# Three fp32 loads in one queue, w_in's first quarter in two loads, and q turned at other places in a decayed-attention and MLP kernel

## The chip, the cores and the metric

The kernel runs on one core of a Trainium2 chip. The time is the device time of one execution in microseconds, given as the median of several runs. TensorE is called PE here, VectorE DVE, ScalarE ACT, GpSimd POOL and SyncE SP, as in the profile.

## The reference

Attention with a decay per head and no softmax, then a two-layer MLP with the snake activation. B, H, S, D = 4, 8, 768, 64; the MLP is 512 to 2048 to 512.

```python
for b in range(nb):                                   # blocks of 64 positions
    intra = einsum('bhic,bhjc->bhij', qb, kb) * Dmask # lam^(i-j) for i >= j
    intra = einsum('bhij,bhjd->bhid', intra, vb)
    inter = einsum('bhid,bhde->bhie', qb * lam_pow, kv_state)
    out[:, :, sl] = intra + inter
    kv_state = lam_block * kv_state + einsum('bhsd,bhse->bhde', kb * rev_pow, vb)
x = out.transpose(0, 2, 1, 3).reshape(B * S, H * D)
h = x @ w_in
g = h + sin(alpha * h)**2 / (alpha + 1e-09)
return g @ w_out
```

## The kernel before

The 768 positions are cut into six chunks of 128 positions (t = 0 to 5). A chunk holds 4 batches × 128 positions = 512 rows. For each chunk the kernel does the attention, which ends in `xt[t]` (the rows' 512 features, turned, in bf16), and then the MLP, group g = t: 16 hidden blocks of 128 features (`hidden(g, f)`, f = 0 to 15, four matmuls each into one PSUM bank `hps`), the activation, and the projection to the output (`project(g, m, part)`: batch m, a quarter of the 16 blocks; `queue_units` puts the projections in a list, and `run(n)` issues the next n of them). There is no scheduler: every engine's order is the order in which the program issues. PE's work of three stages is interleaved by hand: while group g's hidden blocks run, the attention of chunk g + 1 and the projections of earlier groups are put between them.

In `hidden`, ACT makes the sine of a block (L465) and then mostly its square (L470). `squarer(g, f)` says who squares: in group 0 DVE does so for some f, in `finish` (L478). `finish` also makes `gall` from the square and the bank (L479, DVE), and with that the bank is free for a later block. In group 1 the blocks 4 to 14 go round three banks, so that block 12 takes the bank that block 9 had.

Chunk 0 is done with one block of 128 positions, without a state (`scores1`, L307; `outs`, L318). The later chunks have two blocks of 64 and a state: `states` (L378), `update`, `scores` (L398), `masks` (DVE, L405), `outputs_first` (L412), `outputs` (L437), `leave` (L444). q and k have to be turned first: on PE with an eviction by ACT or DVE (`turn`, L282 to L286, one batch; `turns_pair`, L296 to L301, two), or from chunk 2 on mostly by a transposing DMA in SP's queue (`turn_by_dma`).

Loads: nearly everything comes through POOL's software queue, cast from fp32 to bf16 on the way (`load`, `load_w_in`, `load_w_out`). Each such load takes over the landing semaphore of the one eight places ahead in POOL's order, and POOL waits for that one's landing before it issues. Only three pieces for the start come in fp32 through hardware queues: k of batch 0 (`raw["k0"]`), q of batch 0 (`q0`) and k of batch 1 (`k1`) of chunk 0. DVE casts the two k (L525, L533) and multiplies q by the powers `Rq` (L526). `mask_128` makes the table `C0` of the decay, one half per call (L529). Between the steps PE runs fillers (`spin`, L131).

For groups 1 and on, `feed(g)` and `slots(g)` give what is put at each hidden block: feed's steps come ahead of `hidden(g, i)`, slots' steps behind it, and then come the projections and `finish`.

Of the kernel before, what the change touches and what calls it, by code (L numbers as in the profile page):

```python
# [15 lines left out]
def kernel(  # L16
# [11 lines left out]
    nc = tc.nc  # L28
    P = nc.NUM_PARTITIONS
# [28 lines left out]
    def bank(nm, n, dtype=FP32):  # L58
        return psum.tile([P, 512 if dtype is FP32 else 1024], dtype, name=nm, tag=f"b{n}")
# [3 lines left out]
    AB = (4, 5, 6, 7)  # L63
# [7 lines left out]
    qn, kn, vn = {}, {}, {}  # L71
# [4 lines left out]
            d[t] = p.tile([P, B, H, D], BF16, name=nm)  # L76

    raw = {}
    for nm, eng in (("k0", nc.sync), ("q0", nc.scalar), ("k1", nc.sync)):
        raw[nm] = rawp.tile([P, H, D], FP32, name=f"raw_{nm}")  # L80
        eng.dma_start(out=raw[nm][:], in_=NAT[nm[0]][1][int(nm[1]), :, 0:T, :].rearrange("h p e -> p h e"))
    alpha_fp = consts.tile([NFC, P], FP32, name="alpha_fp")
# [4 lines left out]
    def load_w_in(i, w0=0, w1=512):  # L87
        w = slice(512 * i + w0, 512 * i + w1)
        nc.gpsimd.dma_start(out=w_in_sb[i][:, :, w0:w1], in_=moe_w_in[:, w].rearrange("(c p) g -> p c g", p=P))
# [25 lines left out]
    for hs in (slice(0, HP), slice(HP, H)):  # L115
        nc.gpsimd.dma_start(out=vn[0][:, 3, hs, :], in_=v[3, hs, 0:T, :].rearrange("h p e -> p h e"))
    load_w_in(0, 0, P)
    load_w_in(0, P, 2 * P)
    load_w_in(0, 2 * P, 512)
    for i in range(1, 4):  # L120
        load_w_in(i)

# [5 lines left out]
    def spin(n, bk, cols=256):  # L128
        ps = bank("hps", bk)
        for _ in range(n):  # L130
            nc.tensor.matmul(out=ps[:, 0:cols], lhsT=fill[:, 0:P], rhs=fill[:, 0:cols], start=True, stop=True)  # L131
# [79 lines left out]
    V, G, A = nc.vector, nc.gpsimd, nc.scalar  # L211
# [17 lines left out]
    def home(t, blk):  # L229
        return SB[2 if blk else t % 2]  # L230
# [7 lines left out]
    def decay_k(t, b0, b1):  # L238
        if t not in kdec:
            kdec[t] = kdp.tile([P, B, H, D], BF16, name="kdec")  # L240
        R = later["R64" if t else "R128"]
        o = int(turned_by_one(t, b0 // 2))
        nc.gpsimd.tensor_tensor(out=kdec[t][:, b0:b1, :, :], in0=kn[t][:, b0:b1, :, :],  # L243
                                in1=R[:, o:o + H].unsqueeze(1).unsqueeze(3).broadcast_to([P, b1 - b0, H, D]),
                                op=ALU.mult)
# [32 lines left out]
    def turn(t, nm, b, n, eng):  # L278
        src, u = (kn, 0) if nm == "k" else (qn, 1)
        ps = bank("T_ps", n, BF16)[:].rearrange("p (n c i) -> p n c i", n=2, c=HP)[:, u]  # L280
        for hp in range(HP):
            nc.tensor.transpose(out=ps[:, hp, :], in_=src[t][:, b, 2 * hp:2 * hp + 2, :], identity=iden[:])  # L282
        if eng is nc.scalar:
            eng.copy(out=both[t][:, u, b, :, :], in_=ps)  # L284
        else:
            eng.tensor_copy(out=both[t][:, u, b, :, :], in_=ps)  # L286
# [44 lines left out]
    def states1(t, pr, n):  # L331
        ps = bank("KV0_ps", n)[:].rearrange("p (u c d) -> p u c d", u=2, c=HP)
        for h in range(2 * H):
            half, m = where(1, pr, h)
            nc.tensor.matmul(out=ps[halves(half), m // HP, m % HP, :], lhsT=head(kdec, t, pr, h),
                             rhs=vn[t][:, 2 * pr + h // H, h % H, :], start=True, stop=True)
        new_state(1, pr, ps, "first")
# [4 lines left out]
    def decay_state(n, pr):  # L342
        nc.gpsimd.tensor_tensor(out=pair(SD, pr), in0=pair(S_of[n], pr), op=ALU.mult,  # L343
                                in1=L64[:, pr].unsqueeze(1).unsqueeze(3).broadcast_to([P, 2, HP, D]))

    def cast_state(n, pr, dst):
        nc.gpsimd.tensor_copy(out=pair(dst, pr), in_=pair(S_of[n], pr))  # L347
# [102 lines left out]

    def squarer(g, f):
        if g == 0:
            return V if f in (1, 3, 5, 7, 9, 13) else A
        return A

    H0 = (0, 1, 2, 3, 5, 6, 7, 4, 0, 1, 3, 5, 0, 1, 5, 0)
# [1 line left out]
    def hidden(g, f, between=None):  # L458
        hps = bank("hps", H0[f] if g == 0 else (0, 5, 4, 2)[f] if g == 1 and f < 4 else AB[0] if g == 1 and f == 15 else AB[f + 1] if g == 2 and f < 2 else HB[(f + 2) % 3] if g == 1 else HB[(16 * g + f + 1) % 3])
        w = w_in_sb[f // 4]  # L460
        for c in range(NDC):
            nc.tensor.matmul(out=hps[:], lhsT=w[:, c, (f % 4) * P:(f % 4 + 1) * P],  # L462
                             rhs=xt[g][:, c, :], start=(c == 0), stop=(c == NDC - 1))
        s_sb = mlps.tile([P, GRP], BF16, name="s_sb")
        nc.scalar.activation(out=s_sb[:], in_=hps[:], func=ACTF.Sin, scale=alpha_sb[:, f:f + 1])  # L465
        if between:
            between()
        s2 = mlps.tile([P, GRP], BF16, name="s2")
        if squarer(g, f) is A:
            nc.scalar.activation(out=s2[:], in_=s_sb[:], func=ACTF.Square)  # L470
        elif squarer(g, f) is G:
            nc.gpsimd.tensor_tensor(out=s2[:], in0=s_sb[:], in1=s_sb[:], op=ALU.mult)
        hps_of[g, f] = (hps, s_sb, s2)
# [48 lines left out]
    new_xt(0)  # L522
    new_turned(0)
    spin(4, 0, 512)
    nc.vector.tensor_copy(out=kn[0][:, 0, :, :], in_=raw["k0"][:])  # L525
    nc.vector.tensor_tensor(out=qn[0][:, 0, :, :], in0=raw["q0"][:], op=ALU.mult,  # L526
                            in1=Rq[:].unsqueeze(2).broadcast_to([P, H, D]))
    def mask_128(hd):
        nc.vector.tensor_tensor(out=C0[:, hd], in0=tri[:].unsqueeze(1).broadcast_to([P, HP, T]),  # L529
                                in1=NE[:, hd].unsqueeze(2).broadcast_to([P, HP, T]), op=ALU.mult)  # L530

    mask_128(0)
    nc.vector.tensor_copy(out=kn[0][:, 1, :, :], in_=raw["k1"][:])  # L533
    mask_128(1)
    turn(0, "k", 0, 4, A)
    spin(2, 3)
# [68 lines left out]
    def run(n):  # L605
        for _ in range(min(n, len(behind))):
            behind.pop(0)()
# [3 lines left out]
    for f in range(NFC):  # L611
        hidden(0, f)
        if f in (1, 10):
            states1(0, f // 10, 2 if f == 10 else 4)
        if f == 10:
            decay_k(1, 0, 2)
            decay_state(1, 0)
            cast_state(1, 0, home(1, 0))
            load(1, "q", 2, 4)
            load_w_out(2)  # L620
            load_w_out(3)
            load(2, "v", 0, 2)
        if f in (11, 12):
            run(1)
        if f == 12:
            turns_pair(1, "k", 0, 4, (A, A))
            turn(1, "q", 0, 2, A)
            turn(1, "q", 1, 3, V)
        if f == 14:
            scores(1, (0,), (4, 2))  # L630
            masks(1, 0)
        if f == 15:
            run(1)
            states(1, (0,), (3, 4))
            finish(0, 14)
            update(1, 0, 0)
        if f != 14:
            finish(0, f)
# [33 lines left out]
    def slots(g):  # L672
        t = g + 1
        d = {i: [] for i in range(NFC)}
        if g == 1:
            at = dict(KV=5, F=9, O=12)
        else:
            at = dict(KV=4, F=8, O=12)
        d[at["KV"]] += [(states, t)]
        for n in range(4):  # L680
            d[at["KV"] + ((0, 0, 1, 2)[n] if g == 1 else n)] += [(update, t, n // 2, n % 2)]
        if g == 1:
            d[7] += [(turns_pair, 2, "q", 2, AB[0], (A, A))]
        else:
            d[at["F"]] += [(scores, t), (masks, t, 0)]
        d[at["F"] + (g > 1)] += [(masks, t, 1)]
        d[at["O"]] += [(outputs, t), (leave, t, 0)]
        d[at["O"] + (g > 1)] += [(leave, t, 1)]
        return d

    def feed(g):
        t = g + 1
        d = {i: [] for i in range(NFC)}
        if g == 1:
            d[2] += [(turn_by_dma, 2, 0, "k"), (pair_ready, 2, 1), (decay_state, 1, 0), (decay_state, 1, 1), (turn_by_dma, 2, 1, "k"), (turn_by_dma, 2, 0, "q")]
            d[7] += [(put_held,)]
            d[9] += [(scores, 2), (masks, 2, 0)]
        if t + 1 < NT:
            if g == 1:
                d[6] += [(new_chunk, 3)] + [(load, 3, nm, b, b + 2) for nm, b in (("v", 0), ("k", 0), ("v", 2))]  # L700
                d[7] += [(load, 3, nm, b, b + 2) for nm, b in (("k", 2), ("q", 0), ("q", 2))]
            else:
                a = 6 if g == 2 else 2
                d[a] += [(new_chunk, t + 1)] + [(load, t + 1, nm, b, b + 2) for nm, b in (("v", 0), ("k", 0), ("v", 2))]
                d[a + 2] += [(load, t + 1, nm, b, b + 2) for nm, b in (("k", 2), ("q", 0), ("q", 2))]
            d[12] += [(turn_by_dma, t + 1, 0, "k"), (turn_by_dma, t + 1, 1, "k")]
            d[13] += [(pair_ready, t + 1, 0)]
            d[14] += [(turn_by_dma, t + 1, 0, "q"), (turn_by_dma, t + 1, 1, "q")]
            d[15] += [(pair_ready, t + 1, 1)]
        return d  # L710
# [59 lines left out]
```

## Time and profile before

| | |
|---|---|
| median of 3 runs | 209.48 us (209.28 to 209.59) |
| the profiled execution | 209.52 us, of which the span is 207.7 us |
| granted PE clock | 1.0 |
| PE, DVE, ACT, POOL busy | 198.1, 132.5, 143.1, 108.0 us |
| chain that ended last | PE 75%, DMA 12%, POOL 8%, issue 2%, ACT 2% |
| POOL's software queue | 76,720 packets, 13.24 MB |

The profile is of one execution. Busy time is that of instructions on an engine; the share of the chain is what one sees when one follows the last instruction back, step by step, to what released it. In the rows of a timeline stand the start and the length in microseconds, engine, line, operation and tiles, and in brackets how long the engine stood idle ahead of it and for whom.

### The profile page before, as it was taken

Reading aid. Unit: us, or ns where it says so; the run is one execution under the profiler, and the core shown is the slowest. Engines: PE = TensorE matmul, PEld = TensorE weight load, DVE = VectorE, ACT = ScalarE, POOL = GpSimd, SP = SyncE. Lnnn points to the kernel's source line nnn. Section 1 sums busy time; section 2 is a strip of 40 time slices with the busy share of each in tenths; the row PEclk is TensorE's granted clock in tenths of the full one; section 3 lists DMA queues with packets and bytes.
Section 4 is the critical chain, followed back from the end, with each engine's and each line's share of the span. In section 5 each row is a group of like instructions: output and inputs, shape, how many; then the busy total and the mean of one; then the engine's idle time right before and its main releaser. Section 6 shows DMA issues by size and latency. Waiting matters only on the chain.

```text
span 207.7 us, 5323 instructions
## 1 busy us (share of the span) xinstructions
PE 198.1 (95%) x2203; PEld 97.9 (47%) x2233; DVE 132.5 (64%) x219; ACT 143.1 (69%) x240; POOL 108.0 (52%) x113
## 2 busy tenths in 40 slices
PE   7898998999998999999999999999999999999993
PEld 2563444554454544445445444444445444444462
DVE  6895996582897969968557968555867544444000
ACT  4897988323988799675776675776676787887121
POOL 8979959997989983999976940002000000000000
PEclk9999999999999999999999999999999999999999
DMA  7999999999999999599999929601101101110212
GB/s 144 157 159 207 206 160 181 179 183 156 155 264 111 146 151 176 37 170 158 137 149 194 171 60 157 150 0 54 50 3 54 50 0 50 52 54 0 101 60 94
DMA packets 99338, 24.60 MB, mean 118 GB/s; under 512 B 92002, under 2 KB 96370, under 8 KB 99314
## 3 DMA queue, kind: packets, MB, share of 16 engines
q0 software_dynamic: 76720, 13.24, 85.9%
q1 hardware_dynamic: 21552, 10.76, 25.2%
q10 hardware_dynamic: 1042, 0.26, 0.6%
q8 instruction: 17, 0.28, 0.5%
q14 instruction: 7, 0.06, 0.1%
HBM read 27.27 MB, written 6.29 MB: 162 GB/s over the span
## 4 chain that ended last, share of the span: by engine, by line
PE 75%; DMA 12%; POOL 8%; issue 2%; ACT 2%; POOLq 0%; ACTq 0%
PE ops L490 35%; PE hps L462 33%; DMA kn<-in_k_dram 4%; DMA w_out<-in_moe_w_out_dram 4%; DMA vn<-in_v_dram 3%; POOL kdec L243 3%; PE O_ps L412 2%; PE hps L514 2%; PE F_ps L398 1%; POOL qn L104 1%; PE KV_ps L378 1%; PE O_ps L437 1%; POOL kn L104 1%; ACT s_sb L465 1%; POOL qn L101 1%
## 5 line engine op out<-in xcount | busy, mean ns | idle before, releaser
L479 DVE SCALAR_TENSOR_TENSOR gall<-s,r_sb,hps 128x512 bf16<-128x512 bf16 x96 | 70.9, 744 | 43.7 <-ACT s L470 43.4
L462 PE MATMUL hps<-xt,w_in 128*128 128x512 bf16 x370 | 94.3, 379 | 1.5 <-DMA w_in<-in_moe_w_in_dram 0.4
L490 PE MATMUL ops<-w_out,gall 128*128 128x512 bf16 x352 | 90.5, 379 | 1.2 <-issue 0.3
L465 ACT ACTIVATE s_sb<-hps,alpha_sb 128x512 bf16<-128x512 f32 x96 | 65.3, 684 | 33.5 <-PE hps L462 33.1
L470 ACT ACTIVATE s<-s_sb 128x512 bf16<-128x512 bf16 x90 | 56.7, 630 | 2.8
L462 PEld LDWEIGHTS <-w_in 128*128 128x128 bf16 x384 | 36.5, 98 | 43.7 <-DMA w_in<-in_moe_w_in_dram 0.9
L490 PEld LDWEIGHTS <-gall 128*128 128x128 bf16 x368 | 34.7, 98 | 41.2 <-issue 0.9
L243 POOL TENSOR_TENSOR kdec<-kn,R 128x1024 bf16<-128x1024 bf16 x12 | 22.8, 1919 | 3.7 <-DMA kn<-in_k_dram 3.3
L347 POOL CAST sb<-S 128x512 bf16<-128x512 f32 x20 | 12.3, 621 | 20.8 <-DVE S L354 20.8
L343 POOL TENSOR_TENSOR SD<-S,L 128x512 f32<-128x512 f32 x16 | 16.8, 1050 | 8.9 <-DVE S L354 8.7
L444 DVE TENSOR_TENSOR xt<-O_ps,Etab 128x512 bf16<-128x512 f32 x20 | 12.8, 684 | 6.0 <-PE O_ps L437 6.0
L104 POOL DMA_DIRECT2D vn<-in_v_dram x12 | 14.0, 1173 | 0.0
L497 DVE COPY o_sb<-ops 128x512 f32<-128x512 f32 x15 | 10.3, 689 | 4.2 <-PE ops L490 4.1
L499 ACT COPY o_sb<-ops 128x512 f32<-128x512 f32 x8 | 4.6, 576 | 12.0 <-PE ops L490 12.0
L405 DVE TENSOR_TENSOR STm<-F_ps,C 128x512 bf16<-128x512 f32 x20 | 12.7, 683 | 0.2 <-PE F_ps L398 0.2
L354 DVE TENSOR_TENSOR S<-SD,KV_ps 128x512 f32<-128x512 f32 x16 | 10.8, 682 | 0.1
L131 PE MATMUL hps<-fill 128*128 128x256 bf16 (+1 forms) x30 | 8.1, 379 | 1.5 <-DVE fill L124 1.5
L104 POOL DMA_DIRECT2D qn<-in_q_dram x8 | 8.8, 1097 | 0.3 <-issue 0.3
L284 ACT COPY QKT<-T_ps 128x512 bf16<-128x512 bf16 x11 | 6.3, 587 | 3.5 <-PE T_ps L282 3.4
L104 POOL DMA_DIRECT2D kn<-in_k_dram x7 | 7.6, 1092 | 0.0
L412 PEld LDWEIGHTS <-sb 64*64 64x64 bf16 x320 | 4.3, 108 | 4.7 <-issue 4.7
L101 POOL DMA_DIRECT2D kn<-in_k_dram x5 | 6.2, 1234 | 0.0
(76 smaller groups left out, 114.3 us busy)
## 6 DMA issues: line engine op xcount, KB each, us to landing
out_dram<-o_sb SPq DMA_DIRECT2D x23, 256.0 KB, 2.1
vn<-in_v_dram POOLq DMA_DIRECT2D x11, 256.0 KB, 7.7
w_out<-in_moe_w_out_dram POOLq DMA_DIRECT2D x4, 512.0 KB, 11.1
w_in<-in_moe_w_in_dram POOLq DMA_DIRECT2D x3, 512.0 KB, 9.6
kn<-in_k_dram POOLq DMA_DIRECT2D x5, 256.0 KB, 7.6
qn<-in_q_dram POOLq DMA_DIRECT2D x5, 256.0 KB, 8.4
kn<-in_k_dram POOLq DMA_DIRECT2D x5, 240.0 KB, 7.3
qn<-in_q_dram POOLq DMA_DIRECT2D x5, 240.0 KB, 8.0
```

Of the source, the lines that this page charges most:

```text
L104: nc.gpsimd.dma_start(out=to, in_=by_head)
L243: nc.gpsimd.tensor_tensor(out=kdec[t][:, b0:b1, :, :], in0=kn[t][:, b0:b1, :, :], in1=R[:, o:o + H].unsqueeze(1).unsqueeze(3).broadcast_to ...
L343: nc.gpsimd.tensor_tensor(out=pair(SD, pr), in0=pair(S_of[n], pr), op=ALU.mult, in1=L64[:, pr].unsqueeze(1).unsqueeze(3).broadcast_to([P, ...
L347: nc.gpsimd.tensor_copy(out=pair(dst, pr), in_=pair(S_of[n], pr))
L354: nc.vector.tensor_tensor(out=S, in0=pair(SD, pr), in1=ps, op=ALU.add)
L405: nc.vector.tensor_tensor(out=st[:, hd], in0=att["F", t, pr, hd], op=ALU.mult, in1=of_mask(C64, t, pr, hd).unsqueeze(1).broadcast_to([P, 2 ...
L444: nc.vector.tensor_tensor(out=xview(t)[:, 2 * pr:2 * pr + 2, blk, :, :], in0=att["O", t, pr, blk], in1=Eb, op=ALU.mult)
L462: nc.tensor.matmul(out=hps[:], lhsT=w[:, c, (f % 4) * P:(f % 4 + 1) * P], rhs=xt[g][:, c, :], start=(c == 0), stop=(c == NDC - 1))
L465: nc.scalar.activation(out=s_sb[:], in_=hps[:], func=ACTF.Sin, scale=alpha_sb[:, f:f + 1])
L470: nc.scalar.activation(out=s2[:], in_=s_sb[:], func=ACTF.Square)
L479: nc.vector.scalar_tensor_tensor(out=gall[g][:, f, :], in0=s2[:], scalar=r_sb[:, f:f + 1], in1=hps[:], op0=ALU.mult, op1=ALU.add)
L490: nc.tensor.matmul(out=ops[:], lhsT=gall[g][:, f, m * P:(m + 1) * P], rhs=w_out_sb[part][:, f % 4, :], start=(f == 0), stop=(f == NFC - 1))
```

## The change

- The loads of k0, q0 and k1 are all issued on SP, in this order; q0 was issued on ACT.
- w_in's first quarter (512 columns) is loaded as 128 and 384 columns; it was 128, 128 and 256. POOL has one load less to issue, and each later one takes over the semaphore of another load than before.
- DVE casts k0 and k1 one right behind the other, ahead of the multiplication of q0; k1's cast stood between the two halves of the mask table.
- In group 0, block 1 is squared by ACT instead of DVE.
- q of chunk 1, batches 0 and 1, is turned behind hidden block 13 of group 0 instead of block 12, and both evictions are on DVE; the first was on ACT.
- q of chunk 2, batches 2 and 3, is turned by PE ahead of hidden block 7 of group 1 instead of behind it.

```diff
-    for nm, eng in (("k0", nc.sync), ("q0", nc.scalar), ("k1", nc.sync)):
+    for nm, eng in (("k0", nc.sync), ("q0", nc.sync), ("k1", nc.sync)):
...
     load_w_in(0, 0, P)
-    load_w_in(0, P, 2 * P)
-    load_w_in(0, 2 * P, 512)
+    load_w_in(0, P, 512)
...
         if g == 0:
-            return V if f in (1, 3, 5, 7, 9, 13) else A
+            return V if f in (3, 5, 7, 9, 13) else A
...
-    nc.vector.tensor_copy(out=kn[0][:, 0, :, :], in_=raw["k0"][:])
+    for b in range(2):
+        nc.vector.tensor_copy(out=kn[0][:, b, :, :], in_=raw[f"k{b}"][:])
     nc.vector.tensor_tensor(out=qn[0][:, 0, :, :], in0=raw["q0"][:], op=ALU.mult,
...
     mask_128(0)
-    nc.vector.tensor_copy(out=kn[0][:, 1, :, :], in_=raw["k1"][:])
     mask_128(1)
...
         if f == 12:
             turns_pair(1, "k", 0, 4, (A, A))
-            turn(1, "q", 0, 2, A)
+        if f == 13:
+            turn(1, "q", 0, 2, V)
             turn(1, "q", 1, 3, V)
...
-        if g == 1:
-            d[7] += [(turns_pair, 2, "q", 2, AB[0], (A, A))]
-        else:
+        if g > 1:
             d[at["F"]] += [(scores, t), (masks, t, 0)]
...
-            d[7] += [(put_held,)]
+            d[7] += [(put_held,), (turns_pair, 2, "q", 2, AB[0], (A, A))]
```

## The prediction

> **What bounds the kernel now.** I read the page first, then the chain of waits in order of time, then the timeline of the stretches where the chain is not TensorE.
>
> ```profile
> PE 198.1 (95%) x2203; PEld 97.9 (47%) x2233; DVE 132.5 (64%) x219; ACT 143.1 (69%) x240; POOL 108.0 (52%) x113
> ```
>
> TensorE (PE) is busy for 95% of the span, so what can be won is its idle time, and of that only what ends up on the chain. The chain view (start, length, what) runs through loads up to 43.77 and almost only through PE from there on:
>
> ```profile
> 35.22 8.51 DMA w_out<-in_moe_w_out_dram
> 43.77 1.02 PE ops L490 x4
> ```
>
> The third quarter of w_out is issued at 35.22 and lands at 35.22 + 8.51 = 43.73; PE starts on it at 43.77. The timeline shows PE's stops (in brackets the idle time before a row and what ended it):
>
> ```profile
> 20.34 6.22 PE L462 MATMUL hps<-xt,w_in 128*128 128x512 bf16 x27 [0.41 <-DMA w_in<-in_moe_w_in_dram]
> ...
> 31.74 0.62 PE L282 MATMUL T_ps<-iden,qn 128*128 128x128 bf16 x8 [0.57 <-DMA qn<-in_q_dram]
> ...
> 43.77 1.02 PE L490 MATMUL ops<-w_out,gall 128*128 128x512 bf16 x4 [0.18 <-DMA w_out<-in_moe_w_out_dram]
> ...
> 62.81 0.73 PE L398 MATMUL F_ps<-QKT 64*64 64x64 bf16 x64 [0.60 <-ACT QKT L299]
> ```
>
> Up to 43.77 PE waits three times, each time for a load of POOL's software queue: 0.41 + 0.57 + 0.18 = 1.16 us. What loses less than that before 43.77 is swallowed there, and what wins time there is lost again, as long as the third quarter of w_out lands when it does. So I asked the DMA view whether that landing can move, for 5.1 to 43.7 us, and for one microsecond with large and one with small packets:
>
> ```profile
> DMA  9999999999999999999999999999999999999999
> ...
> q0 software_dynamic: 26912, 6.82, 193.1%
> ```
> ```profile
> DMA packets 207, 0.21 MB, mean 209 GB/s; under 512 B 3, under 2 KB 207, under 8 KB 207
> ```
> ```profile
> DMA packets 1234, 0.16 MB, mean 157 GB/s; under 512 B 1234, under 2 KB 1234, under 8 KB 1234
> ```
>
> The 16 DMA engines are busy in every slice (all nines) and the software queue (q0) moves 6.82 MB in that time. It runs full, so a load lands when what is ahead of it has passed, not sooner for being issued sooner. **My reading: up to 43.77 the kernel is paced by the software queue, behind it by PE.**
>
> **The change part by part.**
>
> *One software load less.* The first quarter of w_in comes as 128 + 384 columns instead of 128 + 128 + 256. Bytes are the same; packets go from 512 + 512 to 512. From the two rows above, a packet costs the queue 1 us / 1234 = 0.81 ns at 130 bytes (0.16 MB / 1234) and 1 us / 207 = 4.83 ns at 1,014 bytes (0.21 MB / 207). A line through both rises 4.02 ns over 884 bytes and has a fixed part of 0.22 ns, so 512 fewer packets take 512 × 0.22 = 0.11 us off everything behind them. Bounds: -0.1 (nothing saved, and the larger block in the way of what is behind it) to 0.41 us (512 packets at the full price of a small one). I take 0.11 because both rows are of this queue running full; the landing at 43.73 then comes at 43.62.
>
> On POOL itself one issue goes:
>
> ```profile
> 9.35 3.04 POOL L89 DMA_DIRECT2D w_in<-in_moe_w_in_dram x4
> ...
> 13.28 0.74 POOL L89 DMA_DIRECT2D w_in<-in_moe_w_in_dram x1 [0.88 <-DMA vn<-in_v_dram]
> ...
> 15.68 3.77 POOL L243 TENSOR_TENSOR kdec<-kn,R 128x1024 bf16<-128x1024 bf16 x2
> ```
>
> In the program a software load waits for the landing of the one eight places ahead (it takes over its semaphore). The wait of 0.88 us for v stays, now ahead of the last quarter of w_in instead of the third, so POOL passes 13.28 as before with one issue less to do: kdec starts 0.74 us earlier, at 14.94, and the loads behind it are issued 0.74 us earlier. By the full queue that moves no landing. Price of the merge: the second block of 128 columns must wait for all 384.
>
> ```profile
> L89 POOL DMA_DIRECT2D w_in<-in_moe_w_in_dram x1: 844/844/844, 10.8 to 10.8; - x1
> ...
> DMA to landing us min/median/max: 6.2/6.2/6.2
> ```
> ```profile
> 15.77 1.89 PE L462 MATMUL hps<-xt,w_in 128*128 128x512 bf16 x7
> ```
>
> The rows are the 256 columns' load, landing at 10.8 + 6.2 = 17.0, and the first two blocks on PE. I put the 384 columns at 17.0 less 0.11, 16.9 us. The second block starts at about 15.77 + 1.89/2 = 16.7; alone that would cost 0.2 us, but as follows it starts later than 16.9 anyway.
>
> *The three fp32 loads and the casts.* Now k of batch 0 and k of batch 1 go through SP's queue and q through ACT's:
>
> ```profile
> 0.74 1.08 SPq L81 DMA_DIRECT2D raw_k<-in_k_dram  x2
> ...
> 4.49 0.82 DVE L525 CAST kn<-raw_k 128x512 bf16<-128x512 f32 x1
> ...
> 5.77 0.69 DVE L526 TENSOR_TENSOR qn<-raw_q,Rq 128x512 bf16<-128x512 f32 x1 [0.46 <-ACT Rq L171]
> ...
> 6.98 0.42 DVE L533 CAST kn<-raw_k 128x512 bf16<-128x512 f32 x1
> ...
> 8.22 2.68 DVE L311 TENSOR_TENSOR STm<-F_ps,C 128x512 bf16<-128x512 f32 x4 [0.22 <-PE F_ps L307]
> ...
> 13.94 2.02 DVE L325 TENSOR_TENSOR xt<-O_ps,Etab 128x512 bf16<-128x512 f32 x4
> ```
> ```profile
> DMA to landing us min/median/max: 3.5/4.4/5.4
> ```
> ```profile
> DMA packets 278, 0.07 MB, mean 282 GB/s; under 512 B 278, under 2 KB 278, under 8 KB 278
> ...
> q1 hardware_dynamic: 271, 0.07, 121.2%
> ```
>
> The row of landings is raw_k's, its least and its greatest: batch 0 lands at 0.74 + 3.5 = 4.2, batch 1 at 1.3 + 5.4 = 6.7. Afterwards SP issues k0, q0, k1. The same three times 256 KB have to pass either way and k1 is last in both orders, so I keep its landing at 6.7. The last two rows, of 2.75 to 3.00 us, have SP's queue (q1) almost alone at 282 GB/s, so one queue can fill the engines. At that rate the 512 KB behind k0 pass in 1.9 us: lower bound 4.2 + 1.9 = 6.1. Upper bound, if q0 took as long again as k1 takes from k0's landing (2.5 us): 9.2. 6.7 is near the lower one because of the q1 row. The Trainium skill ("DMA: Bandwidth & Descriptors", section "Issuing engines are not separate DMA queues") says that loads started from several engines run on the same 16 engines and that this saves only issue time; by that rule k1 would come later by one issue at most, 0.5 us. No row here shows three loads in one queue, so the rule is not put to the test by this trace.
>
> But VectorE (DVE), which runs in order, now casts k1 ahead of the multiplication of q. It waits for 6.7, casts until 7.1 and multiplies until 7.8, where it ends at 6.46 today. Behind that instruction wait the turning of q0 on PE (its eviction on ACT, the first scores) and on DVE both masks and all STm.
>
> ```profile
> 7.46 0.40 PE L282 MATMUL T_ps<-iden,kn 128*128 128x128 bf16 x4 [0.32 <-DVE kn L533]
> ```
> ```profile
> 8.22:15.96 7.74, 7.04 (x96) 4.34 (x96) 7.25 (x13) 7.34 (x20) 6.68 (x10) 1.00 2.75 159
> ```
>
> From q's product to the first STm pass 8.22 - 6.46 = 1.76 us today, of which PE's wait of 0.32 for k1 goes: 7.8 + 1.44 = 9.2 to 9.3. From 8.22 to the end of xt (13.94 + 2.02 = 15.96) DVE is busy 7.25 of 7.74 us (the third number of the last row, which is the table by stretches). So xt is ready between 9.3 + 7.25 = 16.55 and 9.3 + 7.74 = 17.0; I take 0.8 us late, the middle, and the first block at 16.6 instead of 15.77. This loss of 0.8 us (bounds 0.2 and 3.3 from k1's bounds) is absorbed: 0.41 us at 20.34, the rest at the second and third stop, of 1.16 us in all.
>
> *The square of block 1 on ACT.* DVE loses one square (L478, 0.42 us), ACT gains one (L470, 0.63 us):
>
> ```profile
> 21.41 0.69 ACT L465 ACTIVATE s_sb<-hps,alpha_sb 128x512 bf16<-128x512 f32 x1 [0.39 <-PE hps L462]
> ...
> 22.31 0.42 DVE L478 TENSOR_TENSOR s<-s_sb 128x512 bf16<-128x512 bf16 x1
> ...
> 29.90 0.69 ACT L465 ACTIVATE s_sb<-hps,alpha_sb 128x512 bf16<-128x512 f32 x1 [0.45 <-PE hps L462]
> ```
> ```profile
> L470 ACT ACTIVATE s<-s_sb 128x512 bf16<-128x512 bf16 x90 | 56.7, 630 | 2.8
> ```
>
> With the late start ACT is 0.8 + 0.63 = 1.4 us late and makes up 0.39 + 0.45 us where it idles today. The 0.6 left are covered by PE's lead: the blocks of this first pass go round eight PSUM banks, so PE needs no bank back for seven blocks. I cost it at nothing; without that cover it would be 0.6 us.
>
> *q of the second chunk, turned one block later and evicted by DVE.* PE no longer stands 0.57 us at 31.74: block 13 fills it, and by 31.9 q has landed. The scores need both evictions, 2 × 0.42 us on DVE, which has nothing else due at 32.3. PE wins 0.57 us here and reaches w_out's third quarter earlier. What is late next is that landing, so what was won is lost at 43.6 again.
>
> *q of the third chunk, turned ahead of block 7 instead of behind it.* The wait of 0.60 us at 62.81 goes. What is late next:
>
> ```profile
> 59.21 0.69 ACT L465 ACTIVATE s_sb<-hps,alpha_sb 128x512 bf16<-128x512 f32 x1 [0.29 <-PE hps L462]
> ...
> 61.70 1.05 ACT L299 COPY QKT<-T_ps 128x512 bf16<-128x512 bf16 x2
> ...
> 64.04 0.75 DVE L479 SCALAR_TENSOR_TENSOR gall<-s,r_sb,hps 128x512 bf16<-128x512 bf16 x1 [1.27 <-ACT s L470]
> ...
> 64.71 2.48 DVE L405 TENSOR_TENSOR STm<-F_ps,C 128x512 bf16<-128x512 f32 x4
> ...
> 67.10 1.40 DVE L479 SCALAR_TENSOR_TENSOR gall<-s,r_sb,hps 128x512 bf16<-128x512 bf16 x2
> ...
> 67.89 1.02 PE L462 MATMUL hps<-xt,w_in 128*128 128x512 bf16 x3
> ```
>
> From 59.21 ACT works without a gap through the sines and squares of blocks 6, 7, 8 and the two evictions until 64.0; changing their order doesn't change that end. DVE then does gall of block 8, four masks, gall of block 9 (to 67.10 + 0.75 = 67.85). Block 12 uses block 9's PSUM bank and starts at 67.89. So PE would wait there what it no longer waits at 62.81: I cost the edit at 0 (bounds: -0.6 if block 12 isn't held, +1.05 if the two evictions, now ahead of block 7's sine, were to hold block 10 in full, which reuses block 7's bank).
>
> **Sum.** The profiled execution took 209.52 us (the span of 207.7 in the table above and 1.8 around it) and lies 0.04 above the median of 209.48. Only the queue's 0.11 us reaches the end: 209.52 - 0.11 = 209.41, on the median's scale 209.37.
>
> **The rivals.**
>
> *Faster: landings follow the issues.* If POOL's 0.74 us did carry over to w_out, PE could use it: it has the 0.57 us of the second stop and 0.18 of the third in hand. 209.48 - 0.74 = 208.7. Against it: every slice of the DMA view is at nine tenths and more. The same time would come out if block 12 were free early (-0.6: 208.9). Together 0.2.
>
> *Slower: k1 lands late.* The stops absorb 1.16 us, the loss is 0.8 with k1 at 6.7; so from 7.1 on each 0.1 us of k1's landing is 0.1 us of the total. At 7.7 it would be 209.48 + 0.6 = 210.1, at the bound of 9.2 it would be 211.6. For it: k1 is now third in one queue, the cast of k0 took 0.82 us where k1's took 0.42, and the software queue starts beside it at about 5 us. Against it: the bytes are the same. Chance 0.2.
>
> *Slower: PE loses its pace.*
>
> ```profile
> 5.91 0.63 PE L131 MATMUL hps<-fill 128*128 128x256 bf16 x2
> ...
> 6.75 0.38 PE L131 MATMUL hps<-fill 128*128 128x256 bf16 x2
> ```
>
> The same pair of fillers takes 0.63 us at 5.91 and 0.38 at 6.75: PE comes up to pace in between, and in the changed kernel it then stands for 1.2 us before q is turned. If it fell back until after the first four blocks, these would take twice their 2 × 1.89 = 3.8 us; less the 1.16 - 0.8 = 0.4 that the stops still hold that is +3.4, 212.9. It decides if the slow pace lasts beyond the first fillers into the blocks. The Trainium skill ("TensorE: Matmul & The Clock Gate", Part 1) puts the fall-back at an idle window of about 3.4 us, longer than the gap here. Chance 0.07.
>
> **How the numbers follow.** Forecast, 209.37 with its own range 209.1 to 209.6 (the packets' bounds and the runs' spread): 0.53. Faster rivals 0.2, slower ones 0.27. The range reaches to 208.75 and 210.1 and leaves out the rest of both sides, under 0.2. A difference of 0.2%, 0.42 us, is about what a measurement of this kernel can tell from none; faster by more 0.2, within 0.53, slower by more 0.27.
>
> **What would show it.** Right: k1's cast starts at 6.7 and q's product ends near 7.8; the first block at 16.6; no stop at 31.74; PE still stops for w_out's third quarter, landing at 43.6; no stop at the scores of 62.81 but one of 0.5 us ahead of block 12. Wrong: that landing moves by more than 0.4 us, PE reaches it after it has landed, or block 12 follows its predecessor without a stop.

## The result: 0.8% slower

The changed kernel takes 211.12 us (210.53 to 212.2, 6 runs), the kernel before, beside it, 209.49 (209.28 to 209.59, 6 runs): a ratio of 1.0083, with an interval of 1.0054 to 1.0112. The forecast was no change. The profiled execution took 212.2 us (span 210.4) and is the longest of the six, so its trace shows a loss of 2.7 us where the median shows 1.6; the mechanism is read from it, the size from the ratio. Its mean granted clock is also the lowest of the six, 0.983 against 0.989 to 0.998.

The page after: the engine line and the chain by engine and line. DMA falls from 12% of the chain to 3%, and all of that 3% is one load, k of batch 1.

```profile
PE 199.4 (95%) x2203; PEld 99.9 (47%) x2233; DVE 132.3 (63%) x219; ACT 142.6 (68%) x240; POOL 107.5 (51%) x112
...
PE 89%; DVE 3%; DMA 3%; issue 2%; ACT 1%; SPq 0%; DVEq 0%; ACTq 0%
```

The chain of waits after, in order of time, begins with that load, which lands at 1.87 + 6.28 = 8.15 us:

```profile
1.87 6.28 DMA raw_k<-in_k_dram
```

The timeline after shows what follows from it (lines of the changed kernel are one or two lower than before):

```profile
8.18 0.77 DVE L525 CAST kn<-raw_k 128x512 bf16<-128x512 f32 x1 [2.87 <-DMA raw_k<-in_k_dram]
8.87 0.67 DVE L526 TENSOR_TENSOR qn<-raw_q,Rq 128x512 bf16<-128x512 f32 x1
...
9.60 0.61 PE L281 MATMUL T_ps<-iden,qn 128*128 128x128 bf16 x4 [3.56 <-DVE qn L526]
10.00 0.63 PE L130 MATMUL hps<-fill 128*128 128x256 bf16 x2
...
19.96 1.89 PE L461 MATMUL hps<-xt,w_in 128*128 128x512 bf16 x7
...
45.97 1.03 PE L489 MATMUL ops<-w_out,gall 128*128 128x512 bf16 x4
...
64.70 0.74 PE L397 MATMUL F_ps<-QKT 64*64 64x64 bf16 x64
...
69.80 0.66 PE L411 MATMUL O_ps<-QKT,sb 64*64 64x64 bf16 x59 [0.38 <-DVE STm L404]
```

VectorE stands 2.87 us for k1, so q's product ends at 9.54 (6.46 before) and TensorE stands 3.56 us ahead of q's turn. Then TensorE is slow: four turns take 0.61 us and two fillers 0.63, where the row of fillers before, quoted in the prediction, shows 0.38 at 6.75. The table by stretches says for how long (the columns are stretch, length, then busy time and count of PE, PEld, DVE, ACT, POOL, then the granted clock, the DMA share, GB/s):

```profile
5.38:8.79 3.41, 0.66 (x7) 0.38 (x6) 0.61 (x1) 1.06 (x5) 3.41 (x5) 1.00 2.05 170
8.79:12.20 3.41, 2.60 (x25) 2.10 (x26) 2.52 (x5) 1.40 (x4) 3.10 (x5) 0.50 2.44 155
12.20:15.62 3.42, 3.39 (x35) 2.35 (x32) 2.24 (x5) 2.91 (x8) 2.18 (x4) 0.50 1.83 181
15.62:19.00 3.38, 3.30 (x48) 2.03 (x46) 3.30 (x7) 3.08 (x10) 3.38 (x2) 1.00 1.26 206
```

From 8.79 to 15.62 the granted clock is 0.5, right behind a stretch in which TensorE was busy for 0.66 of 3.41 us. At half clock for 6.83 of 210.4 us the mean loses 0.016, which is most of what the 0.983 lacks; one stretch of 3.41 us costs it 0.008. The first hidden block comes at 19.96 instead of 15.77, 4.19 us late. After that nothing stops TensorE for a load: w_out's third quarter is there before its unit starts at 45.97, and the stops at 20.34, 31.74 and 43.77 are gone. The second group's first block, in the same timelines of both kernels, tells how much of the 4.19 us they swallow:

```profile
49.60 1.89 PE L462 MATMUL hps<-xt,w_in 128*128 128x512 bf16 x7
```
```profile
52.16 1.89 PE L461 MATMUL hps<-xt,w_in 128*128 128x512 bf16 x7
```

The upper row is of the kernel before. From first block to first block it needs 49.60 - 15.77 = 33.83 us, the changed one 52.16 - 19.96 = 32.20. So 4.19 - 1.63 = 2.56 us of lateness are left, and they stay to the end (2.7 in the span). The 4.19 have two parts: q's turn on TensorE starts at 9.60 instead of 6.52, 3.08 us late, and from there to the first block pass 10.36 us instead of 15.77 - 6.52 = 9.25.

### The profile page after: what moved, and what is told of

Read it like the earlier page. It is cut to its first block, busy times and chain, and to the rows that moved or that the text cites. A ratio compares the mean times of both kernels' runs of the same rounds, so it can differ in the third digit from the quotient of the medians.

```text
span 210.4 us, 5322 instructions
## 1 busy us (share of the span) xinstructions
PE 199.4 (95%) x2203; PEld 99.9 (47%) x2233; DVE 132.3 (63%) x219; ACT 142.6 (68%) x240; POOL 107.5 (51%) x112
## 3 DMA queue, kind: packets, MB, share of 16 engines
HBM read 27.27 MB, written 6.29 MB: 159 GB/s over the span
## 4 chain that ended last, share of the span: by engine, by line
PE 89%; DVE 3%; DMA 3%; issue 2%; ACT 1%; SPq 0%; DVEq 0%; ACTq 0%
PE hps L461 38%; PE ops L489 37%; DMA raw_k<-in_k_dram 3%; PE O_ps L411 2%; PE T_ps L281 2%; PE hps L513 2%; PE KV_ps L377 1%; PE O_ps L436 1%; PE F_ps L397 1%; PE hps L130 1%; DVE STm L404 1%; PE F_ps L306 1%; PE T_ps L295 1%; PE O_ps L317 1%; DVE S L357 1%
## 5 line engine op out<-in xcount | busy, mean ns | idle before, releaser
L469 ACT ACTIVATE s<-s_sb 128x512 bf16<-128x512 bf16 x91 | 57.3, 630 | 2.9
L342 POOL TENSOR_TENSOR SD<-S,L 128x512 f32<-128x512 f32 x16 | 16.9, 1061 | 10.5 <-DVE S L353 10.4
L283 ACT COPY QKT<-T_ps 128x512 bf16<-128x512 bf16 x10 | 5.7, 586 | 7.7 <-PE T_ps L281 7.7
L104 POOL DMA_DIRECT2D kn<-in_k_dram x7 | 7.6, 1089 | 0.0
L281 PE MATMUL T_ps<-iden,qn 128*128 128x128 bf16 x32 | 3.6, 260 | 3.6 <-DVE qn L526 3.6
```

Source lines behind the costliest of these rows:

```text
L104: nc.gpsimd.dma_start(out=to, in_=by_head)
```

## The experiments

My theory after this result: the loss is made in the first 16 us alone. k1 lands late and its cast stands in front of q's product; TensorE starves for 3.56 us and loses its clock. The rivals: the other edits cost too; or the pace alone, or the late k1 alone, makes the loss. Ratios are against the kernel before in the same set of runs.

### The start, undone in parts

**Cast of k1 back behind q's product**, loads still all on SP.

```diff
-    for b in range(2):
-        nc.vector.tensor_copy(out=kn[0][:, b, :, :], in_=raw[f"k{b}"][:])
+    nc.vector.tensor_copy(out=kn[0][:, 0, :, :], in_=raw["k0"][:])
...
     mask_128(0)
+    nc.vector.tensor_copy(out=kn[0][:, 1, :, :], in_=raw["k1"][:])
     mask_128(1)
```

> The changed kernel with one thing undone: DVE casts k of batch 1 between the two mask halves again, as before the change; all three fp32 loads stay in SP's queue. Theory A (the multiplication of q stands behind a cast that waits for k1's landing at 8.2, PE idles 3.6 us and falls to half pace for two of its clock windows): q's product is made at 5.8 again, PE is not idle for more than 2 us, its clock stays at 1.0, the first STm is at about 9.3 because k1 still lands late, the first hidden block at about 16.8, and the total 209.4 (209.0 to 209.8). Rival B (one of the other edits, w_in, the square or the two turns, costs the 1.6 us): 211 as the changed kernel.

Measured: 210.05 us, 1.0029 [1.0008, 1.005]. k1 is as late as in the changed kernel, but q is not behind it:

```profile
5.73 0.69 DVE L525 TENSOR_TENSOR qn<-raw_q,Rq 128x512 bf16<-128x512 f32 x1 [0.42 <-ACT Rq L170]
...
8.17 0.77 DVE L532 CAST kn<-raw_k 128x512 bf16<-128x512 f32 x1 [1.16 <-DMA raw_k<-in_k_dram]
...
17.01 1.89 PE L461 MATMUL hps<-xt,w_in 128*128 128x512 bf16 x8
...
49.22 1.89 PE L461 MATMUL hps<-xt,w_in 128*128 128x512 bf16 x8
```

The first block comes 1.24 us late, and by 49.22 the profiled run is 0.38 ahead. Its ten runs lie between 209.04 and 211.31, so the profiled one (209.13) is among the best. What the others lost no trace shows, but their mean clocks do: three with 1.0 took 209.04 to 209.32, six with 0.989 to 0.992 took 209.64 to 210.4, and the one with 0.984 took 211.31. Two thirds of the loss go with this one cast; what is left goes with the clock, which most of these runs still lost.

**q0 on ACT's queue**, casts adjacent as in the change.

```diff
-    ... ("q0", nc.sync) ...
+    ... ("q0", nc.scalar) ...
```

> The changed kernel with q of batch 0 loaded through ACT's queue again; DVE still casts k1 ahead of the multiplication. Theory A: k1 lands at 6.7 as before the change, q's product ends at 7.8, PE idles 1.3 us and keeps its clock, the first hidden block is at 16.6 and the stops for loads swallow it: 209.4 (209.0 to 209.8). Rival B: 211. Rival C (the order on DVE alone costs it, whenever k1 lands): 210.5 to 211 with the clock lost all the same.

Measured: 209.72 us, 1.0014 [0.9999, 1.003].

```profile
6.72 0.61 DVE L525 CAST kn<-raw_k 128x512 bf16<-128x512 f32 x1 [1.41 <-DMA raw_k<-in_k_dram]
7.25 0.67 DVE L526 TENSOR_TENSOR qn<-raw_q,Rq 128x512 bf16<-128x512 f32 x1
...
17.57 1.89 PE L461 MATMUL hps<-xt,w_in 128*128 128x512 bf16 x8
...
49.78 1.89 PE L461 MATMUL hps<-xt,w_in 128*128 128x512 bf16 x8
```

With two hardware queues k1 lands at 6.70, as the prediction had it, and q's product ends at 7.92 (predicted 7.8); TensorE stands 1.46 us ahead of q's turn. The first block is still 1.80 us late, 0.97 more than predicted for it, and the table by stretches shows why:

```profile
6.38:9.79 3.41, 1.72 (x27) 1.37 (x26) 2.72 (x5) 1.61 (x4) 3.41 (x5) 1.00 2.53 153
9.79:13.20 3.41, 3.26 (x34) 2.23 (x32) 2.42 (x5) 2.94 (x8) 2.72 (x5) 0.50 3.35 148
```

The clock falls here too, for one stretch. The 1.63 us of stops swallow nearly all of it. By their mean clocks, eight of the ten runs lost a stretch (0.989 to 0.992: 209.62 to 210.53 us) and two did not (1.0: 208.9 and 209.0). So a lost stretch costs some 0.8 us, and it is lost even with k1 on time.

**The start alone**, in the kernel before: three loads on SP, casts adjacent.

```diff
-    ... ("q0", nc.scalar) ...
+    ... ("q0", nc.sync) ...
...
+    for b in range(2):
+        nc.vector.tensor_copy(out=kn[0][:, b, :, :], in_=raw[f"k{b}"][:])
...
-    nc.vector.tensor_copy(out=kn[0][:, 1, :, :], in_=raw["k1"][:])
```

> The kernel before with only the start of the change: three fp32 loads in SP's queue and both casts ahead of the multiplication of q. Theory A: the whole loss is here, 211 (210.5 to 212.5), PE at half pace for some microseconds from about 9 on, first hidden block near 20. Rival B: 209.5.

Measured: 211.34 us, 1.0102 [1.0087, 1.0118]. In this trace TensorE never came up to pace before 14.85, where the record of the granted clock begins; the table by stretches shows 1.00 ahead of that, but the rows show the slow pace:

```profile
9.72 0.61 PE L282 MATMUL T_ps<-iden,qn 128*128 128x128 bf16 x4 [3.18 <-DVE qn L527]
...
12.93 0.61 PE L307 MATMUL F_ps<-QKT 64*128 64x128 bf16 x8
...
14.87 0.40 PE L307 MATMUL F_ps<-QKT 64*128 64x128 bf16 x8
...
19.73 1.89 PE L462 MATMUL hps<-xt,w_in 128*128 128x512 bf16 x8
```
```profile
8.00:11.40 3.40, 1.68 (x16) 1.35 (x18) 2.23 (x4) 0.97 (x3) 3.15 (x5) 1.00 2.43 155
```

So a mean clock near 1 does not prove that the start was fast. **Everything but the start** (the changed kernel with this diff turned round):

> The changed kernel with the start of before (q0 through ACT's queue, k1's cast between the mask halves); w_in in two loads, the square of block 1 on ACT and both turns as in the change. Theory A: no loss; the third quarter of w_out lands 0.1 to 0.7 us earlier and PE follows it: 209.4 if the merge is worth 0.1, 208.8 if it is worth 0.7. Rival B: 211.

Measured: 209.22 us, 0.9998 [0.9985, 1.0012]. The whole loss is in the start; the rest together can't be told from nothing. This kernel differs from the one with q0 on ACT in the order of the casts alone, and all its ten runs have a mean clock of 0.997 or more: with k1 on time, it is the order of the casts that loses the clock.

**The changed kernel with TensorE kept at work**: 24 fillers instead of 2 between the turns of k0 and of q0.

```diff
     turn(0, "k", 0, 4, A)
-    spin(2, 3)
+    spin(24, 3)
     turn(0, "q", 0, 5, A)
```

> The changed kernel with 24 fillers on PE instead of 2 between the turn of k of batch 0 and the turn of q of batch 0, where PE stands 3.6 us in the changed kernel; nothing else is different. Theory A1 (most of the loss is PE's pace, which falls because PE stands): the clock stays at 1.0, the first hidden block comes at 18.0 to 18.5 instead of 19.96, total 209.8 to 210.3. Rival A2 (the late landing of k1 alone does it, PE's pace costs little): 211 as the changed kernel, although the clock is at 1.0.

Measured: 210.38 us, 1.0037 [1.0024, 1.0049], so 0.46% less than the change with nothing but fillers added.

```profile
7.54 0.67 DVE L525 CAST kn<-raw_k 128x512 bf16<-128x512 f32 x1 [2.22 <-DMA raw_k<-in_k_dram]
...
8.12 0.67 DVE L526 TENSOR_TENSOR qn<-raw_q,Rq 128x512 bf16<-128x512 f32 x1
...
9.45 0.39 PE L281 MATMUL T_ps<-iden,qn 128*128 128x128 bf16 x4
...
18.18 1.89 PE L461 MATMUL hps<-xt,w_in 128*128 128x512 bf16 x8
```
```profile
5.00:10.00 5.00, 5.00 (x38) 3.88 (x37) 2.78 (x5) 1.67 (x6) 5.00 (x7) 1.00 2.15 170
10.00:15.00 5.00, 4.11 (x64) 3.04 (x61) 3.85 (x8) 4.80 (x14) 3.90 (x6) 1.00 2.30 164
```

The clock does not fall, and all five runs have a mean of 0.998 or more. k1 landed 0.6 us earlier in this profile than in that of the change, but the fillers last beyond q's product (8.79), so q's turn starts at 9.45, only 0.15 us earlier than there. From q's turn to the first block pass 18.18 - 9.45 = 8.73 us instead of 10.36: with q equally late, the pace alone was worth 1.63 us in the profiled run of the change. By the medians, 0.46 of 0.83%, it was a good half of the loss. The rest is q's late turn.

### Why k1 is late

The view of DMA queues between 4.25 and 5.75 us, while k1 is under way, before and after (packets, MB, share of 16 engines; q0 is POOL's software queue, q1 SP's, q10 ACT's):

```profile
q1 hardware_dynamic: 797, 0.20, 80.8%
q0 software_dynamic: 462, 0.06, 61.4%
q10 hardware_dynamic: 163, 0.04, 15.4%
```
```profile
q0 software_dynamic: 789, 0.10, 103.7%
q1 hardware_dynamic: 481, 0.12, 48.2%
```

After, the software queue moves 789 packets in this stretch instead of 462, and SP's 481 instead of 797. The records of packets have the software queue's first one at 3.84 us instead of 5.05, though POOL issues its first load at 1.34 in both. The same split runs through all the profiles: in the eight kernels with two hardware queues (the one before among them) that first packet comes at 4.62 to 5.18 and k1 lands at 6.6 to 6.9; in the four with one, and POOL left alone, it comes at 3.79 to 3.91 and k1 lands at 7.5 to 8.6. The rival: a third load in one hardware queue is late by itself. To tell them apart I held POOL back with a table that nobody uses.

```diff
+    later = consts.tile([P, 640], FP32, name="later")
+    nc.gpsimd.iota(out=later[:], pattern=[[1, 640]], base=0, channel_multiplier=-1,
+                   allow_small_or_imprecise_dtypes=True)
     for nm, b0, b1 in (("q", 1, 2), ("k", 2, 3), ...
```

> The changed kernel, and POOL makes a second table of positions (128 x 640 elements, used by nobody) ahead of its first software load, which by the 0.23 us of the 128 x 128 one should hold POOL's queue back by about 1.1 us. Theory (the software queue gets in beside k1 because only one hardware queue runs): its first packet comes about 1.1 us later, near 4.9, k1 lands near 7.0 to 7.3 instead of 8.15, q's product ends near 8.3, the first hidden block starts at 17.0 to 17.8, ratio 1.001 to 1.004 with whatever the later issues cost. Rival (three loads in one hardware queue are slow by themselves): k1 still lands at 8.0 or later, the first block at 19.5 or later, ratio 1.008 or more.

Measured: 211.36 us, 1.0097 [1.0062, 1.0131]. A miss: the table took 0.66 us and moved POOL's first issue by 0.30 only, the first packet to 4.06. k1 was no earlier (its cast starts at 8.46). Too small a dose to speak for either side; so the same with 128 × 2048 elements:

> The changed kernel, and POOL makes an unused table of 128 x 2048 elements ahead of its first software load. The table of 640 columns took 0.66 us, that of 128 columns 0.23, so this one should take 1.9 to 2.0 us and POOL's first issue start at about 2.9 instead of 1.34, the first software packet come near 5.3 instead of 3.84. Theory (software queue beside k1): k1 lands at 6.7 to 7.2. Then q's product ends near 8.2 and the first block starts at 16.9 to 18, unless the later software loads hold it. Rival (third load in one hardware queue late by itself): k1 still lands at 8.0 to 8.5.

Measured: 209.93 us, 1.002 [1.0002, 1.0038].

```profile
1.87 0.88 SPq L81 DMA_DIRECT2D raw_k<-in_k_dram x1
...
2.81 1.08 POOL L104 DMA_DIRECT2D qn<-in_q_dram x1
...
6.52 0.43 DVE L529 CAST kn<-raw_k 128x512 bf16<-128x512 f32 x1 [0.61 <-DMA raw_k<-in_k_dram]
6.86 0.68 DVE L530 TENSOR_TENSOR qn<-raw_q,Rq 128x512 bf16<-128x512 f32 x1
...
16.35 1.02 PE L465 MATMUL hps<-xt,w_in 128*128 128x512 bf16 x3
18.72 1.04 PE L465 MATMUL hps<-xt,w_in 128*128 128x512 bf16 x4 [1.35 <-DMA w_in<-in_moe_w_in_dram]
```

POOL's issue comes 1.47 us later, the first software packet at 5.00, and k1, still third in SP's queue, lands at 6.49: earlier than before the change. The first block is at 16.35, 8.75 us behind q's turn at 7.60; the pace was kept, and all ten runs have a mean clock of 0.997 or more. In this profile it still loses two stops for loads of the queue that was held back: 1.35 us at 18.72 for w_in's 384 columns and 0.67 at 44.73 for w_out's third quarter. And with three tables in a row, for k1's landing alone:

> The same with three such tables one behind the other: first software issue near 6.5, first packet near 9 us. k1 then has the engines to itself. Theory: k1 lands at 6.1 to 6.5, the lower bound of the prediction (512 KB behind k0 at 282 GB/s). Rival: 8.0 or later even so. The total is expected 3 to 5 us longer, because every software load comes later; this run is for k1's landing alone.

Measured: 214.76 us in one run; k1 landed at 6.29, with no software packet before 8.42. So the third load of one queue is not late by itself; the software queue beside it makes it late. That is shown. Why that queue starts 1.2 us sooner when ACT's queue is not in use, the runs don't settle. In the eight profiles with q0 on ACT its first packet comes within 0.4 us of the last packet of ACT's queue, on either side of it (5.05 and 5.14 before), as if it got in only when that queue was running dry. The Trainium skill ("DMA: Bandwidth & Descriptors", section "Queues, rings and completion order") has each DMA engine go round the queues that have work for it; by that the software queue would have no one to wait for once its descriptors are ready, and no run here shows when they are.

### The other edits, one by one

**The merged load of w_in, alone** in the kernel before:

```diff
-    load_w_in(0, P, 2 * P)
-    load_w_in(0, 2 * P, 512)
+    load_w_in(0, P, 512)
```

> The kernel before with only w_in's first quarter in two loads instead of three. By the prediction's price of a packet (0.11 us) w_out's third quarter lands at 43.6 and the total is 209.25. By the landings of the run with only the rest of the change it lands 0.6 to 0.9 us earlier, at 42.9 to 43.1, and since nothing else is changed PE is still held 0.57 us at the turn of q of the second chunk, so it can use some 0.5 us: 208.8. Rival: nothing is won (209.35) because something behind 43.8 is late next.

Measured: 209.81 us, 1.0007 [0.9997, 1.0017].

```profile
18.45 1.04 PE L461 MATMUL hps<-xt,w_in 128*128 128x512 bf16 x4 [1.66 <-DMA w_in<-in_moe_w_in_dram]
```

**q of the second chunk, alone:**

```diff
         if f == 12:
             turns_pair(1, "k", 0, 4, (A, A))
-            turn(1, "q", 0, 2, A)
+        if f == 13:
+            turn(1, "q", 0, 2, V)
             turn(1, "q", 1, 3, V)
```

> The kernel before with only the turn of q of the second chunk moved behind block 13 and both evictions on DVE. As predicted: the stop of 0.57 us at 31.7 goes, PE waits that much longer for w_out's third quarter at 43.8, total 209.35 (209.2 to 209.5). Rival: 208.8, if the 0.57 us reach the end.

Measured: 209.16 us, 0.9981 [0.9968, 0.9995].

```profile
43.28 1.02 PE L490 MATMUL ops<-w_out,gall 128*128 128x512 bf16 x4 [0.55 <-DMA w_out<-in_moe_w_out_dram]
```

**q of the third chunk, alone:**

```diff
-        if g == 1:
-            d[7] += [(turns_pair, 2, "q", 2, AB[0], (A, A))]
...
-            d[7] += [(put_held,)]
+            d[7] += [(put_held,), (turns_pair, 2, "q", 2, AB[0], (A, A))]
```

> The kernel before with only the turn of q of the third chunk moved ahead of block 7. As predicted: the stop of 0.60 us at the scores near 62.8 goes and one of 0.5 to 0.6 us appears ahead of block 12, which waits for the bank of block 9; total 209.35 (209.2 to 209.5). Rival: 208.75, if block 12 isn't held.

Measured: 209.63 us, 1.0005 [0.9996, 1.0014].

```profile
67.33 0.66 PE L412 MATMUL O_ps<-QKT,sb 64*64 64x64 bf16 x59 [0.38 <-DVE STm L405]
```

**Both turns** (the last two diffs together):

> The kernel before with the two moved turns of q alone (second chunk behind block 13 with both evictions on DVE, third chunk ahead of block 7). Each by itself gave 0.9981 and 1.0005. If they add: 0.9985 to 0.999. If the third chunk's turn gains its 0.6 us once the second chunk's turn has given PE a lead: 0.996. PE should not stop at 31.8 nor ahead of the scores of 62.3, but 0.4 us ahead of block 12 of the second group.

Measured: 209.1 us, 0.998 [0.9971, 0.999]. **Both turns and block 1's square on ACT:**

> The kernel before with the two moved turns and the square of block 1 on ACT: everything but the start and the merged load. If the square costs nothing, as costed, the ratio is that of the two turns alone within 0.001; if ACT's 0.63 us reach PE through the banks, it is 0.003 higher. The kernel with all but the start gave 0.9998, so if this one is at 0.998 the merged load is what takes the rest.

Measured: 209.23 us, 0.9983 [0.9975, 0.9992]. Both beat the kernel before and the changed one. The square costs nothing that can be told (0.9983 against 0.998). Everything but the start was at 0.9998, in another set of runs; the merged load is the only edit between these, but the difference of 0.0015 is about as large as the intervals, so no loss by it is shown.

## Why the prediction was wrong, step by step

**k1's landing, kept at 6.7: the step that failed.** It landed at 8.15. "The same three times 256 KB have to pass either way" left out that the software queue shares the engines and may begin at another time: it began at 3.84 instead of 5.05. The range of 6.1 to 9.2 held the value; I chose the end near the row in which SP's queue ran almost alone, and that row would have held only with the software queue still silent, as the run with three tables shows (6.29). With k1 at 6.70 (q0 on ACT) the rest of the change gave 1.0014, which can't be told from no change, as forecast. By the rule of the Trainium skill ("DMA: Bandwidth & Descriptors", section "Issuing engines are not separate DMA queues") k1 would come later by its issue alone; its issue was 0.6 us later (1.87 against 1.26), but its landing 1.5 later. The first half of that rule, that all loads interleave on the same engines, is what the two queue views show.

**From k1 to the first block.** The chain was right where k1 was on time and the pace was kept: the run with POOL held back has q's product ending at 7.54 and the first block 8.81 us later; predicted were 7.8 and 8.8. With q0 on ACT, k1 on time but one stretch lost, the first block came 9.65 behind the product. In the changed kernel the product ended at 9.54, 1.74 later than predicted, and the first block came 10.42 behind it, 1.62 more. The first is k1's landing and its slower cast (0.77 us instead of 0.42), the second the clock, as the run with fillers shows (1.63).

**The rivals.** "k1 lands late" and "PE loses its pace" were priced as alternatives, 0.2 and 0.07; they came together, the late landing making the gap longer. At 8.15 the first gives 209.48 + 1.05 = 210.5; that the second made the rest to 211.1 is argued, not measured. The second was put at nothing in the sum because the gap, 1.2 us with k1 at 6.7, was far from 3.4. That was wrong twice: the gap hangs on k1, so the chances did too, and even with k1 at 6.70 and a gap of 1.46 us (q0 on ACT) most runs lost the clock. Its price was too high: 3.4 us assumed the first four blocks at half pace, but the lost stretches lay ahead of the blocks and cost 1.6. The Trainium skill ("TensorE: Matmul & The Clock Gate", Part 1) puts the fall-back at an idle window of some 3.4 us; the stretches above last 3.41 us, and the clock fell after one with 0.66 us of work, but also after one with 1.72, so here it took no idle window.

**What the stops absorb.** Predicted 1.16 us, measured 33.83 - 32.20 = 1.63. Part of the difference is a fourth wait, for w_out's first quarter: it landed at 27.91, and the projection that needs it started at 27.96, 0.23 us later behind the block ahead of it than in the changed kernel (27.96 - 26.86 against 31.27 - 30.40). The same 32.2 us stand between the first blocks of the two groups in the runs with the cast moved back (49.22 - 17.01) and with q0 on ACT (49.78 - 17.57): that is TensorE without a stop. So a first block up to 17.4 is free in a profile, and the change had gone 2.56 past that.

**w_out's third quarter as a fixed gate: wrong.** It landed at 43.73 before, at 43.24 with q of the second chunk moved alone, at 42.84 with all but the start. So what that turn wins is not all lost there: 0.4 us come through (0.9981), where I had costed 0. What moves the landing is open: POOL's issue moved by only 0.13 us in the first of these, and with q of the third chunk moved alone, an edit that acts later, the landing was 43.49, so some 0.2 us of it may be scatter.

**The merged load.** Costed as a gain of 0.11 us, with the 384 columns landing at 16.9. Alone they landed at 18.41 and TensorE stood 1.66 us for them; most of that was given back at the later stops, and 1.0007 can't be told from nothing. The merging need not be what made them late: in the run with everything but the start, also merged, they landed at 16.64, and in two runs with three loads (q of the third chunk alone; both turns and the square) the last 256 columns came at 18.41 and 18.50 instead of 16.99. In the changed kernel they landed at 17.22, and the late start hid it.

**Block 1's square and q of the third chunk: right.** Both cost nothing. The stop at 62.81 went, and in its place 0.38 us came up ahead of the outputs for a mask, just before block 12, where I had looked for 0.5 at block 12's bank: VectorE did gall of block 8, the four masks and gall of block 9, as argued, and TensorE stopped for the last mask, one instruction ahead of that gall.

## What to carry to other kernels

Moving a load to another queue can move when the other queues get their share; ask of each queue not only what is ahead in it, but when the others start. A step put in front of another on an engine that runs in order makes that other wait for the step's latest input too: here one cast ahead of q's product turned 1.5 us of DMA into 3.1 us for TensorE. And where an engine's gap grows with an uncertain landing, the price of a lost clock belongs to the same case as the late landing, not beside it. Read the pace from the rows and from the clock of every run: one profile of a kernel that loses its clock in some runs can be a lucky or an unlucky one.

## What the runs showed of the hardware that I had not expected

The granted clock fell to 0.5 after a stretch with 1.72 us of TensorE work in 3.41 (q0 on ACT), but not in the following two, of the runs with the cast moved back and with POOL held back. Each stretch is counted from where the run's record of the granted clock begins (6.38, 8.00 and 4.74):

```profile
7.99:11.40 3.41, 2.05 (x34) 1.61 (x35) 2.90 (x5) 1.89 (x5) 3.41 (x5) 1.00 2.51 155
11.40:14.80 3.40, 3.08 (x51) 2.15 (x48) 3.29 (x7) 3.34 (x12) 2.08 (x4) 1.00 2.29 165
```
```profile
4.74:8.15 3.41, 1.70 (x17) 0.91 (x16) 2.75 (x9) 1.92 (x6) 3.41 (x5) 1.00 2.01 154
8.15:11.56 3.41, 2.61 (x44) 2.03 (x44) 2.95 (x5) 3.26 (x10) 3.41 (x5) 1.00 2.09 133
```

So the stretch need not be wholly idle, and busy time alone (1.72 falls, 1.70 doesn't) doesn't decide. The record begins at 4.74 to 8.00 in most profiles, so the same gap can fall differently into the stretches of two runs. That this makes the scatter is argued; what is on record is that the ten runs with the cast moved back lie 2.3 us apart and sort by their mean clock, as shown above, where the 25 before in the same set lie 0.6 apart. The changed kernel's six lie 1.7 apart: 0.983 for the longest, four at 0.989 to 0.991 (210.53 to 211.35), and one at 0.998 (211.66), perhaps a start like that of the run with the start alone, which no trace shows.

A POOL instruction can hold VectorE. The timeline of the run with POOL held back (one table of 128 × 2048), of POOL and of VectorE:

```profile
1.03 1.83 POOL L114 IOTA later<- 128x2048 f32 x1
```
```profile
1.46 1.48 DVE L137 TENSOR_SCALAR iden<-dist 128x128 bf16<-128x128 f32 x1
```

VectorE's small `iden` takes 1.48 us there, to 2.94, just past the table's end at 2.86; before it took 0.15, and beside the shorter table, which ended at 1.69, 0.31, to 1.77. The cast of k0 starts at 5.10 instead of 4.49 for it, so this kernel pays for the held queue with 0.6 us on VectorE, which k1's landing at 6.49 hides.
